# Loading each 4 MB tile of the K and V caches as two transfers of 64 partitions in a one-core attention decode step

## The chip, the core and the metric

The kernel runs on one core of a Trainium2 chip. The metric is the device time of one execution in microseconds; before the change it is 378.08 us, the median of 3 runs (378.05 to 378.56). The profile is one further execution of the same program, with its own span.

## The reference

One decode step for four sequences: layer norm, attention of 32 query heads over 16 cached key/value heads in a window of the last 4096 positions, a residual, a second layer norm and a gated feed-forward layer. What matters here is the size of the caches' window: 4 sequences x 16 heads x 4096 positions x 128 values of two bytes are 67 MB of K and as much of V. Both are read once.

```python
def _A_ref(x, k_cache, v_cache, wq, wo):
    W = min(4096, max(256, Sk // 4))          # 4096 of Sk = 16384
    rep = Hq // Hkv                           # 32 // 16
    q = (x @ wq).reshape(B, Sq, Hq, Dh).transpose(0, 2, 1, 3)
    k = jnp.repeat(k_cache[:, :, Sk - W:, :], rep, axis=1)
    v = jnp.repeat(v_cache[:, :, Sk - W:, :], rep, axis=1)
    scores = jnp.einsum("bhqd,bhkd->bhqk", q, k) * (Dh ** -0.5)
    p = _softmax(scores, axis=-1)
    o = jnp.einsum("bhqk,bhkd->bhqd", p, v)
    return o.transpose(0, 2, 1, 3).reshape(B, Sq, Hq * Dh) @ wo

h = x + _A_ref(_layernorm(x), A_k_cache, A_v_cache, A_wq, A_wo)
h2 = h + _B_ref(_layernorm(h), B_W_gate, B_W_up, B_W_down)   # (relu(h W_gate) * (h W_up)) W_down
```

## The kernel before

The caches are worked on in 16 tiles of K and 16 tiles of V (`NTILE`). Tile g holds four heads of one sequence (g // 4 is the sequence). It is 128 partitions x 16384 values of two bytes, 4 MB, and comes by a single transfer (lines 235 to 242). Partition 4p + a holds positions 128p to 128p + 127 of the window of head a of the four, so one partition's row is one unbroken run of 32 KB in the cache.

A tile lives in one of four slots (`NSLOT`) of a big buffer, `arena`, in a ring (`ring_slot`, line 229). The order of the loads is wq, K tiles 0 to 3, then K tile g and V tile g - 4 in turn, and V tiles 12 to 15 (lines 251 to 264). Then the weights of the output projection and of the feed-forward layer follow, in the same buffer (lines 265 to 284). All of these are issued by SP on one queue, in this order. `place` (line 216) records which 64-value blocks of the arena a load overwrites, and makes the load wait for the last instruction that reads them: the scores of the earlier K tile, `("QK", g)`, or the weighted sum of the earlier V tile, `("PV", g)`.

The order on each engine is that of the program text. `Prog.emit` (line 71) gives every instruction that somebody waits for a semaphore value. For a transfer the value of its semaphore grows by 16 (line 92), one for each of the 16 DMA engines; each slot has one semaphore (`slot0` to `slot3`). A wait that an engine has already made is not made again (line 108).

On the computing side a K tile is first rearranged in place by VectorE (`turn_k`, line 418; the transpose is line 422), and then TensorE makes the scores (`pe_qk`, lines 425 to 448, and the helper at line 34). A V tile goes straight to TensorE (`pe_pv`, line 492, whose matmuls are line 507 and line 34). Between them lie the softmax (lines 450 to 489) and the selection of the valid part of the product (`select_o`, lines 512 to 525). The weights need TensorE alone and a few small operations on VectorE and ScalarE (lines 606 to 702).

The small input x comes by a transfer of its own, 4 partitions of 1152 bytes, issued by ScalarE (line 335).

Of the kernel before, what the change touches and what calls it, by code (L numbers as in the profile page):

```python
# [16 lines left out]
SK = 16384  # L17
WIN = 4096
# [7 lines left out]
TILE = 16384  # L26
# [94 lines left out]
def bass_sequential_preLN__sliding_block_cached__glu_gated_reglu__decode_kernel(  # L121
# [12 lines left out]
    with ExitStack() as es:  # L134
        cnt = [0]

        def sb(name, shape, dt):
            return es.enter_context(nc.sbuf_tensor("sb_" + name, shape, dt))

        P = Prog()  # L140
# [8 lines left out]
        arena = sb("arena", [128, AW], BF16)  # L149
# [66 lines left out]
        def place(name, off, size, reader, make, key=None):  # L216
            deps = []
            for blk in range(off // 64, (off + size) // 64):
                r = owner.get(blk)
                if r is not None and r not in deps:  # L220
                    deps.append(r)
                owner[blk] = reader
            semk = key or "d_" + "_".join(str(v) for v in name)
            P.dma("sync", ("L",) + name, make, semk, deps)
            land[name] = off

        ring = [(-1 - 2 * NTILE) % NSLOT]
# [1 line left out]
        def ring_slot():  # L229
            s = ring[0] % NSLOT  # L230
            ring[0] += 1
            return s


        def add_kv(kind, g):
            b, qd = divmod(g, 4)
            s = ring_slot()
            off = slot0 + s * TILE
            cache = A_k_cache if kind == "K" else A_v_cache
            src = cache[b, 4 * qd:4 * qd + 4, SK - WIN:SK, :].rearrange("a (p t) d -> p a (t d)", p=32)  # L240
            place((kind, g), off, TILE, ("QK", g) if kind == "K" else ("PV", g),
                  lambda e: e.dma_start(out=arena[:, off:off + TILE], in_=src), key=f"slot{s}")  # L242


        def main_rows(W):
            return W[0:512, :].rearrange("(p r) n -> p (r n)", r=4)

        def last_rows(W):
# [3 lines left out]
        s = ring_slot()  # L252
        wq_off = slot0 + s * TILE
        place(("wq", 0), wq_off, TILE, "QMM",
              lambda e: e.dma_start(out=arena[:, wq_off:wq_off + TILE], in_=main_rows(A_wq)), key=f"slot{s}")  # L255
        for g in range(NTILE):
            add_kv("K", g)
            if g >= 4:
                add_kv("V", g - 4)
# [3 lines left out]
        for g in range(NTILE - 4, NTILE):  # L263
            add_kv("V", g)
        place(("wo",), WO_OFF, H * D, "WO",
              lambda e: e.dma_start(out=arena[:, WO_OFF:WO_OFF + H * D], in_=A_wo.rearrange("(p r) n -> p (r n)", p=128)))
        gu_off = {}
        off = WO_OFF + H * D
        for g, W in ((0, B_W_gate), (1, B_W_up)):
            for m, n, src in ((4, F // 2, last_rows(W)), (0, 3 * F, main_rows(W)[:, 0:3 * F]), (3, F, main_rows(W)[:, 3 * F:4 * F])):  # L270
                if g == 0 and m == 0:
                    n, src = 4 * F, main_rows(W)
# [7 lines left out]
        for r0, r1 in zip(WD_ROWS, WD_ROWS[1:]):  # L280
            place(("wd", r0), wd_off + r0 * D, (r1 - r0) * D, ("DOWN", 1),
                  lambda e, r0=r0, r1=r1: e.dma_start(  # L282
                      out=arena[:, wd_off + r0 * D:wd_off + r1 * D],
                      in_=B_W_down.rearrange("(p r) n -> p (r n)", p=128)[:, r0 * D:r1 * D]))
# [18 lines left out]
                                                in_=c_qm[:, :, :].rearrange("p q (h j) -> p q h j", j=4),  # L303
# [4 lines left out]
                                                in_=to_v[:, :, :].rearrange("p n (k a) -> p n k a", a=4),  # L308
# [14 lines left out]
        for sg in range(2):  # L323
            pool(f"c_toq{sg + 1}", lambda e, sg=sg: e.affine_select(
                out=toq[:, :, :, :], in_=toq[:, :, :, :],
# [213 lines left out]
        def finish_o():  # L539
            for q in range(4):  # L540
                for qd in range(4):
# [17 lines left out]
                                              in_=bass.AP(tensor=e8, offset=0, ap=[[8, 128], [0, 4], [1, 8]])), ["c_e8", "c_selc0"])  # L559
# [47 lines left out]
        for a in range(8):  # L607
            for n in range(2):
                for j in range(4):
# [4 lines left out]
                    else:  # L614
# [6 lines left out]
                                             in_=bass.AP(tensor=psb, offset=512 + 224, ap=[[4096, 128], [1, 64], [0, 2]])), ["part1"])  # L621
# [27 lines left out]
        for g in range(2):  # L649
            for c in (4, 0, 1, 2, 3):  # L650
                part_ = c if c == 4 or (c == 3 and g) else 0
                for m in range(3):
                    for j in range(4):
                        first = m == 0 and j == 0 and (c in (0, 4) or part_ == 3)
                        deps = [("L", "gu", g, part_)] if first else []
# [20 lines left out]
        for i in range(2):  # L676
            dve(("HHT", i), lambda e, i=i: e.transpose(
                out=hhT[:, 576 * i:576 * i + 576].rearrange("p (r q) -> p r q", q=32),
                in_=bass.AP(tensor=pp, offset=3712 + 18 * i, ap=[[PPW, 128], [1, 18], [36, 32]])), [("HH", m) for m in range(3)])
# [12 lines left out]
        for r in range(36):  # L692
            for n in range(2):
                deps = []
# [9 lines left out]
        for n in range(2):  # L704
            lo, hi = ncol[n]
            P.dma(("sync", "scalar")[n], ("O", n), lambda e, n=n, lo=lo, hi=hi: e.dma_start(
                out=orow[:, lo:hi], in_=out_sb[32 * n:32 * n + 4, 0:hi - lo]),
# [31 lines left out]
```

## Time and profile before

| What | Value |
|---|---|
| median of 3 runs | 378.08 us |
| span of the profiled execution | 376.5 us |
| mean TensorE clock granted | 0.79 |
| read from HBM in the span | 159.58 MB, 424 GB/s |
| of these, K and V | 32 transfers of 4096 KB |
| VectorE waiting for K tiles (line 422) | 66.5 us in 16 waits |
| SP waiting for TensorE before loads of line 242 | 237.4 us in 24 waits, the longest 17.4 us |

The profile's page gives busy times and shares by engine, the span in 40 slices, the DMA queues, and the chain of work that ended last. A line such as "L422 DVE" is an instruction of VectorE from line 422 of the program; PE is TensorE, SPq the issuing of transfers by SP. "A <-B" behind an idle time says that the engine was waiting for B. The trace has further records behind the page: for every DMA packet its start, length, size and queue, and for every transfer the sixteen moments at which its semaphore was raised, one by each DMA engine, here called its landings. Times are from the start of the span.

### The profile page before, as it was taken

How to read it: one execution, taken by the hardware profiler on the slowest of the kernel's cores; microseconds unless marked ns; L12 is line 12 of the kernel's file. 1: busy time of each engine (PE TensorE's matmuls, PEld its weight loads, DVE VectorE, ACT ScalarE, POOL GpSimd, SP SyncE). 2: the span in 40 equal slices, each digit the busy share in tenths (PEclk: the TensorE clock that was granted, in tenths of full speed). 3: DMA queues.
4: the chain of work that ended last, by engine and by line, in shares of the span. 5: the costliest groups of instructions: out<-in, count | busy, mean ns of one | idle time of the engine just before them, and what ended most of it. 6: DMA issues, size and time to landing. Idle time of an engine off the chain costs nothing.

```text
span 376.5 us, 2541 instructions
## 1 busy us (share of the span) xinstructions
PE 209.2 (56%) x1447; PEld 39.2 (10%) x694; DVE 227.6 (60%) x164; ACT 53.8 (14%) x84; POOL 10.7 (3%) x29
## 2 busy tenths in 40 slices
PE   0404443249919091749282844664555687776748
PEld 0000000001101010101010100110000101003305
DVE  3088878779292959584847778665659423342140
ACT  3093000211000114010101140101010401121010
POOL 8300000000000000000000000000000000000000
PEclk9975666659979687788778885968596989996688
DMA  8999999999999999999999999999999999999996
GB/s 335 446 435 432 413 446 446 425 411 446 444 421 414 443 444 421 414 446 446 421 413 446 446 418 421 438 446 418 425 439 446 413 432 435 430 423 426 437 414 263
DMA packets 6514, 159.74 MB, mean 424 GB/s; under 512 B 736, under 2 KB 872, under 8 KB 1512
## 3 DMA queue, kind: packets, MB, share of 16 engines
q1 hardware_dynamic: 6488, 159.58, 98.8%
q8 instruction: 8, 0.13, 0.1%
q10 hardware_dynamic: 16, 0.01, 0.0%
q14 instruction: 2, 0.02, 0.0%
HBM read 159.58 MB, written 0.00 MB: 424 GB/s over the span
## 4 chain that ended last, share of the span: by engine, by line
DMA 62%; DVE 18%; PE 18%; SPq 1%; issue 1%; ACT 0%
DMA sb_arena<-in_A_k_cache_dram 53%; DVE sb_arena L422 16%; PE psb L34 11%; DMA sb_arena<-in_B_W_down_dram 9%; PE psb L446 4%; PE psb L507 2%; DVE sb_o_tmp L520 1%; DVE sb_pp L485 1%; PE psb L685 0%; SPq L242 0%; PE psb L473 0%; SPq L282 0%; ACT sb_out_sb L702 0%; SPq L255 0%; SPq L251 0%
## 5 line engine op out<-in xcount | busy, mean ns | idle before, releaser
L422 DVE STREAM_TRANSPOSE sb_arena<-sb_arena 128x8192 f32<-128x8192 f32 (+1 forms) x19 | 139.9, 7365 | 66.5 <-DMA sb_arena<-in_A_k_cache_dram 66.5
L446 PE MATMUL psb<-sb_arena 128*32 128x512 bf16 x256 | 42.5, 629 | 119.1 <-DVE sb_arena L422 119.0
L34 PE MATMUL psb<-sb_arena,sb_pp 128*128 128x512 bf16 x382 | 105.2, 383 | 2.7 <-issue 2.6
L507 PE MATMUL psb<-sb_arena,sb_pp 128*128 128x512 bf16 x115 | 44.1, 383 | 8.9 <-DVE sb_o_tmp L520 8.9
L34 PE MATMUL psb<-sb_arena 128*32 128x512 bf16 x256 | 44.2, 649 | 0.0
L517 ACT COPY sb_o_tmp<-psb 32x512 f32<-32x512 f32 x32 | 18.5, 577 | 179.3 <-PE psb L34 179.1
L520 DVE TENSOR_TENSOR sb_o_tmp<-psb,sb_fm 32x512 f32<-32x512 f32 x32 | 21.7, 678 | 16.9 <-PE psb L34 16.4
L446 PEld LDWEIGHTS psb<-sb_arena 128*32 128x32 bf16 x256 | 9.6, 119 | 161.4 <-DVE sb_arena L422 132.2
L507 PEld LDWEIGHTS psb<-sb_arena,sb_pp 128*128 128x128 bf16 x128 | 12.6, 99 | 113.4 <-issue 113.4
L524 DVE TENSOR_REDUCE sb_o_sel<-sb_o_tmp 128x128 f32<-128x512 f32 x16 | 17.7, 1106 | 0.5
L465 ACT ACTIVATE sb_pp<-psb,sb_hx 128x1024 bf16<-128x1024 f32 x4 | 4.5, 1113 | 78.4 <-DVE sb_hx L462 78.4
L485 DVE TENSOR_TENSOR sb_pp<-psb,sb_m 128x1024 bf16<-128x1024 f32 x8 | 9.4, 1209 | 4.5 <-PE psb L473 4.5
L480 ACT ACTIVATE sb_pp<-psb,sb_m 128x512 bf16<-128x512 f32 x16 | 9.7, 692 | 14.8 <-PE psb L473 14.8
L523 DVE TENSOR_TENSOR sb_o_tmp<-sb_o_tmp,sb_fm 64x512 f32<-64x512 f32 x16 | 11.0, 690 | 0.5
L413 ACT COPY sb_arena<-sb_q_keep 32x256 bf16<-32x256 bf16 x8 | 9.7, 1452 | 0.1
L685 PE MATMUL psb<-sb_arena,sb_pp 128*32 128x352 bf16 (+1 forms) x72 | 7.6, 349 | 3.7 <-DMA sb_arena<-in_B_W_down_dram 3.6
L399 DVE CAST sb_pp<-psb 128x512 bf16<-128x512 f32 x1 | 2.4, 2426 | 11.3 <-PE psb L379 11.3
L468 DVE STREAM_TRANSPOSE sb_pp<-sb_pp 128x1024 bf16<-128x1024 bf16 x4 | 5.0, 1246 | 5.1 <-ACT sb_pp L465 5.1
L473 PE MATMUL psb<-sb_pp,sb_to_v 128*32 128x256 bf16 x64 | 4.3, 401 | 6.2 <-DVE sb_pp L468 6.2
L673 DVE TENSOR_TENSOR sb_pp<-psb,sb_pp 128x384 bf16<-128x384 f32 x3 | 1.5, 551 | 9.0 <-PE psb L664 9.0
L379 PE MATMUL psb<-sb_arena,sb_xnT 128*32 128x512 bf16 x16 | 2.6, 628 | 7.2 <-DMA sb_arena<-in_A_wq_dram 7.2
L664 PE MATMUL psb<-sb_arena,sb_hnT 128*32 128x384 bf16 x40 | 4.2, 405 | 3.9 <-DVE sb_hnT L645 2.0
(119 smaller groups left out, 88.1 us busy)
## 6 DMA issues: line engine op xcount, KB each, us to landing
sb_arena<-in_A_k_cache_dram SPq DMA_DIRECT2D x16, 4096.0 KB, 26.2
sb_arena<-in_A_v_cache_dram SPq DMA_DIRECT2D x16, 4096.0 KB, 28.5
sb_arena<-in_A_wo_dram SPq DMA_DIRECT2D x1, 4608.0 KB, 26.2
sb_arena<-in_B_W_gate_dram SPq DMA_DIRECT2D x1, 4608.0 KB, 29.3
sb_arena<-in_A_wq_dram SPq DMA_DIRECT2D x1, 4096.0 KB, 12.9
sb_arena<-in_B_W_up_dram SPq DMA_DIRECT2D x1, 3456.0 KB, 30.3
sb_arena<-in_B_W_down_dram SPq DMA_DIRECT2D x1, 2160.0 KB, 29.6
sb_arena<-in_B_W_down_dram SPq DMA_DIRECT2D x1, 1440.0 KB, 32.6
```

The costliest lines, as they stand in the source:

```text
L34: return e.add_instruction(mybir.InstMatmult(name=e.bass.get_next_instruction_name(), engine=mybir.EngineType.PE, ins=[e.lower_ap(rhs), e. ...
L413: act("QW", lambda e, i=i, q=q: e.copy(out=bass.AP(tensor=arena, offset=32 * i * AW + 2 * i + q, ap=[[AW, 32], [512, 16], [136, 4], [32, 4]]),
L422: dve(("TRA", g), lambda e: e.transpose(out=dst, in_=src), [("L", "K", g)] if lo == 0 else [])
L446: fn = lambda e, out_=out_, lhsT=lhsT, rhs=rhs, start=start, stop=stop: e.matmul(out_, lhsT=lhsT, rhs=rhs, start=start, stop=stop, skip_gr ...
L480: act(("EV", b, 0), lambda e, a=a: e.activation(out=bass.AP(tensor=pp, offset=2 * a, ap=[[PPW, 128], [8, 2], [32, 128], [1, 2]]), in_=bank ...
L485: dve(("EV", b, 1), lambda e, n=n: e.tensor_tensor(out=bass.AP(tensor=pp, offset=16 + 8 * n, ap=[[PPW, 128], [32, 128], [2, 4], [1, 2]]), ...
L507: fn = lambda e, lhsT=lhsT, rhs=rhs, k=k, j=j: e.matmul(bank[2 + j], lhsT=lhsT, rhs=rhs, start=(k == 0), stop=(k == 7), skip_group_check=True)
L517: act(("OSC", g), lambda e, j=j: e.copy(out=o_tmp[32 * j:32 * j + 32, 0:512], in_=bank[2 + j][32 * j:32 * j + 32, :]), [("PV", g), ("OSEL" ...
L520: dve(("OSD", g), lambda e, j=j: e.tensor_tensor(out=ot(32 * j, 32), in0=bank[2 + j][32 * j:32 * j + 32, :].rearrange("p (t d) -> p t d", ...
L523: dve(("OS", g), lambda e: e.tensor_tensor(out=ot(64, 64), in0=ot(64, 64), in1=fmb(64, 64), op=ALU.mult), [("OSC", g)])
L524: dve(("OSEL", g), lambda e: e.tensor_reduce(out=o_sel[:, qd, b, :], in_=o_tmp[:, 0:512].rearrange("p (t d) -> p d t", d=DH), axis=AX.X, o ...
L685: return lambda e: e.matmul(bank[n][32 * n:32 * n + 32, 0:hi - lo], lhsT=lhsT, rhs=w[:, lo:hi], start=start, stop=stop, skip_group_check=True)
```

## The change

`add_kv` makes two transfers of each tile: partitions 0 to 63 and then partitions 64 to 127, each 2 MB. The rearrangement of the source is split into h (which half), p (16 in place of 32) and t, so each partition gets the same row of the cache as before. `place` takes a list of transfers as well as a single one; the transfers of a list are put on SP's queue one after the other with the same dependencies and the same semaphore. The name of the load stands for the second of them, whose semaphore value counts both (32 for a tile). The loads of the weights and of x are as they were.

```diff
@@ def place(name, off, size, reader, make, key=None):
             semk = key or "d_" + "_".join(str(v) for v in name)
-            P.dma("sync", ("L",) + name, make, semk, deps)
+            for one in make if isinstance(make, list) else [make]:
+                P.dma("sync", ("L",) + name, one, semk, deps)
             land[name] = off
@@ def add_kv(kind, g):
-            src = cache[b, 4 * qd:4 * qd + 4, SK - WIN:SK, :].rearrange("a (p t) d -> p a (t d)", p=32)
+            src = cache[b, 4 * qd:4 * qd + 4, SK - WIN:SK, :].rearrange("a (h p t) d -> h p a (t d)", h=2, p=16)
             place((kind, g), off, TILE, ("QK", g) if kind == "K" else ("PV", g),
-                  lambda e: e.dma_start(out=arena[:, off:off + TILE], in_=src), key=f"slot{s}")
+                  [lambda e, h=h: e.dma_start(out=arena[64 * h:64 * h + 64, off:off + TILE], in_=src[h])
+                   for h in range(2)], key=f"slot{s}")
```

## The prediction

> **What bounds the kernel now.** I read the busy slices and the DMA queues first, then the chain of waits, then single lines. The page:
>
> ```profile
> span 376.5 us, 2541 instructions
> PE 209.2 (56%) x1447; PEld 39.2 (10%) x694; DVE 227.6 (60%) x164; ACT 53.8 (14%) x84; POOL 10.7 (3%) x29
> DMA  8999999999999999999999999999999999999996
> ...
> q1 hardware_dynamic: 6488, 159.58, 98.8%
> ...
> DMA 62%; DVE 18%; PE 18%; SPq 1%; issue 1%; ACT 0%
> ```
>
> No compute engine is busy for more than 60% of the span. The queue that carries every load has its sixteen DMA engines in work for 98.8% of it. So the kernel lasts as long as its bytes take; the DVE and PE pieces of the chain are the path by which a buffer comes free for the next load, not work that delays the bytes. Busy times by stretch, with the granted clock, the DMA share and the rate as the last three columns, agree:
>
> ```profile
> core 0: us, PE busy (x) PEld busy (x) DVE busy (x) ACT busy (x) POOL busy (x), PEclk, DMA share, GB/s
> ...
> 64.00:160.00 96.00, 54.99 (x357) 8.08 (x159) 67.63 (x41) 12.36 (x22) 0.00 (x0) 0.77 1.00 431
> 160.00:326.00 166.00, 101.42 (x580) 14.04 (x231) 104.68 (x70) 19.40 (x34) 0.00 (x0) 0.81 1.01 433
> ```
>
> The rate is the same whatever the clock and the other engines do. The pace of one tile shows in VectorE's first transposes, each of which starts when its K tile has landed:
>
> ```profile
> 23.91 8.71 DVE L422 STREAM_TRANSPOSE sb_arena<-sb_arena 128x8192 f32<-128x8192 f32 x1 [1.03 <-DMA sb_arena<-in_A_k_cache_dram]
> 33.61 8.71 DVE L422 STREAM_TRANSPOSE sb_arena<-sb_arena 128x8192 f32<-128x8192 f32 x1 [0.99 <-DMA sb_arena<-in_A_k_cache_dram]
> 43.33 8.71 DVE L422 STREAM_TRANSPOSE sb_arena<-sb_arena 128x8192 f32<-128x8192 f32 x1 [1.00 <-DMA sb_arena<-in_A_k_cache_dram]
> ```
>
> 9.7 us apart. The landing records give it for all 32 K and V tiles: the first engine is done with wq at 13.62 us and with the last V tile at 324.44 us, 310.82 / 32 = 9.713 us a tile. The packet records say why: one row of a tile is one packet of 32768 bytes, its median time is 1.216 us and its shortest 1.213; 128 rows over 16 engines are 8 packets an engine, 8 x 1.216 = 9.73 us. Packets stand end to end. From the last V tile (all engines at 326.19 us) to the end, the weights queued behind it take 48 us and the close about 2 us.
>
> How deep the queue is decides what SP's issues cost:
>
> ```profile
> L242 SPq DMA_DIRECT2D sb_arena<-in_A_k_cache_dram x16: 534/535/692, 1.7 to 251.4; - x16
> L242 SPq DMA_DIRECT2D sb_arena<-in_A_v_cache_dram x16: 534/535/536, 46.3 to 297.4; - x16
> ...
> DMA to landing us min/median/max: 17.9/26.5/40.2
> ```
>
> An issue takes 0.535 us, and its tile lands 17.9 us later at the least. Of these the tile's own transfer is 9.7, so at least 8.2 us of earlier packets lie ahead of any issue.
>
> **The change, part by part.** Removed: 32 transfers of 128 rows. Added: 64 transfers of 64 rows, with the same bytes, the same rows of the cache to the same partitions, and the same 32 KB packets. Nothing moves on TensorE, VectorE, ScalarE or GpSimd.
>
> SP: 32 more issues of 0.535 us and the step of 0.04 us between issues in the chain, 18.4 us of SP's time. Cover: SP waits 237.4 us for PE at line 242 alone, and the second half needs no wait of its own, since both halves have the same dependencies. A second half goes out 0.58 us late against at least 8.2 us of queued packets, so 0. Behind it on SP stand only later loads. Without that cover it would be the whole 18.4 us.
>
> Semaphores: each transfer ends on each engine with a 4-byte packet of 9 ns. 32 more of them are 0.3 us on every engine. The consumers wait for the sum of both halves (32 a tile), so no transpose or matmul starts sooner than now.
>
> The packets: this is the term that decides, and no K or V row of the trace shows it. A transfer of 64 rows, if it is spread over 16 engines as the transfer of 128 is, has 4 rows an engine, and all sixteen engines write into one half of the partitions at once. The lower end: the limit of 1.216 us sits in the engine that sends. Then a half tile takes 4.86 us and the tile 9.73 as before, cost 0. The instruction fetches of 8192 bytes ahead of the kernel, which don't go to the arena, took 307 ns, 26.7 GB/s, nearly the 26.9 GB/s of 32768 / 1.216. That fits a sender's limit. The upper end: the limit sits where the rows are received, and belongs to a group of partitions. 16 x 26.9 = 431 GB/s into 128 partitions are 3.4 GB/s a partition; 64 partitions take 216 GB/s, a packet 2.43 us, a tile 19.4 us. The nearest row with few partitions is x, 4 rows of 1152 bytes: its four packets took 146, 255, 102 and 48 ns on four engines, all between 2.85 and 3.16 us, so 4608 bytes in 0.305 us, 15.1 GB/s for four engines, 3.8 GB/s a partition. Packets of the same size in the last W_down load, into 128 partitions, took 51 ns. x comes at the start, where other packets are slow too (4096 bytes in 159 to 656 ns), so it is a hint, no measurement. But its rate lies beside the upper end's and a quarter of what four senders alone would give, and I take the upper end.
>
> The upper end has a discount. Two engines that share a receiver lose nothing while one of them is already in the other half. If one leads its partner by w us of work, a half tile costs 2 x 4.86 - w. The sixteen engines finish the first K tile within 0.54 us of each other, two engines taken at random 0.2 us apart; at the last V tile it is 1.75 and 0.82 us, since each of eight 16 KB instruction fetches (about 1.07 us) held up one engine more. A tile is ready when its slowest pair is, so I take the small lead: 64 x 0.2 = 13 us. With 0.82 it would be 52, with 1.75 it would be 112.
>
> [...]
>
> Where the stall goes: into VectorE's wait for K. The first K tile would land near 33 instead of 23.9 us, and the computation of a tile (8.7 us of transpose, 4 us of scores) hides under a load of 19 us, so the next buffer is always free in time and the queue stays full: three tiles lie ahead of each issue. After the last V tile the same weights follow at the same rate, full transfers of 128 rows, 48 us. PE is then ahead of its work of now, not behind.
>
> Sum, against the profiled span: 376.5 + 310.8 (every tile twice as long) - 13 + 0.3 = 674.6. The median lies 378.08 - 376.5 = 1.6 us above the span, so 676 us.
>
> **The rivals.** (B) The receiver is shared, but the engines fall out of step by several us, because one of a pair is favoured or is held up by fetches, and half tiles overlap in part. For it: the spread of landings grows from 0.54 to 1.75 us through the run, and the queue is deep enough that a leader isn't stopped. Against: engines differ only by whole fetch stalls, packets otherwise agree within 1%, and a leader that runs out of issued tiles waits for its partner, which sets them level again. With a lead of half a half tile, 2.43 us, the cost is 310.8 - 64 x 2.43 = 155, time 533 us; the case reaches from 379 to 577.
>
> (C) The packet's limit is the sender's. For it: the 26.7 GB/s of the instruction fetch, and 1.213 us as a hard floor in 4224 packets. Against: x. The time is 378.08 + 0.3 = 378.4 us, not slower by what can be measured. It decides wherever the first half tile lands within 5 us of the transfer ahead of it. That the change doesn't do what it says, since the queue joins both halves, has the same time.
>
> (D) Shorter bursts keep the packets at their floor: 32 tiles x 8 x (1.216 - 1.213) = 0.8 us, time 377.3, faster. Nothing speaks for it but that the floor exists.
>
> **How the numbers follow.** Doubling (577 to 698): 0.62. B: 0.20. C: 0.14. D: 0.04. The forecast is 676 us. Its own range ends above at the full doubling, 376.5 + 310.8 + 0.3 + 1.6 = 689.2, and with each of eight fetches holding up the slowest pair (8 x 1.07 = 8.6) at 698; below at the discount for 1.75 us, 577. To hold 8 in 10, I go down through B to 400, which leaves out C, D and about a tenth of B: 0.62 + 0.18 = 0.80. A measurement of this kernel can tell 0.2%, 0.76 us, from no change. Faster by that: 0.04; within: 0.14; slower: 0.82.
>
> **What would show it.** If right: 32768-byte packets near 2.4 us, the rate near 220 GB/s from the first K tile to the last V tile and 430 after it, the DMA share still at 1.00, transposes of the first K tiles some 19 us apart, K landing some 60 us after issue, and VectorE's wait for K well above its 66.5 us in sum. If packets stay at 1.216 us, the receiver isn't the limit and I am wrong altogether. If packets are bimodal, 1.2 and 2.4, the engines fall out of step and B holds. If the DMA share falls, SP's issues have come onto the path, which I have costed at nothing.

## The result, and the profile after

The changed kernel takes 699.62 us, the median of 4 runs (690.62 to 703.73), against 378.08 (378.05 to 378.56). The comparison, from which disturbed runs are left out, gives a ratio of 1.8333 (95% interval 1.8284 to 1.8382). The profiled execution has a span of 695.2 us, 318.7 us more than before.

The page of the changed kernel: the span, the busy times, the busy share of the DMA engines and the rate in 40 slices, and the queue of the loads.

```profile
span 695.2 us, 2588 instructions
PE 240.0 (35%) x1462; PEld 41.5 (6%) x694; DVE 228.5 (33%) x164; ACT 53.6 (8%) x84; POOL 10.5 (2%) x29
DMA  9999999999999999999999999999999999999997
GB/s 332 213 211 222 216 217 211 215 213 210 211 211 211 212 213 214 211 219 219 211 217 212 213 211 211 217 214 217 211 217 215 213 210 211 215 213 214 420 416 332
...
q1 hardware_dynamic: 7000, 159.59, 99.5%
```

No compute engine has become the limit: VectorE has 228.5 us of work in place of 227.6, and TensorE's 240.0 us in place of 209.2, at a lower granted clock (0.69 in place of 0.79), are 35% of the span. The DMA engines are as full as they were, and move half as much in a microsecond. The low rate begins after the first slice (wq is a whole transfer) and ends in the 38th, where the weights, again whole transfers, come at 420 GB/s. The busy share alone would not have shown anything; it has to be read beside the rate.

The transposes of the first K tiles, from the timeline of VectorE in the changed kernel (start, duration, and in brackets the idle time before and who ended it), and below it VectorE's wait for K in sum, times and longest, and the issues of line 243 (242 before):

```profile
33.80 8.71 DVE L424 STREAM_TRANSPOSE sb_arena<-sb_arena 128x8192 f32<-128x8192 f32 x1 [11.40 <-DMA sb_arena<-in_A_k_cache_dram]
53.52 8.71 DVE L424 STREAM_TRANSPOSE sb_arena<-sb_arena 128x8192 f32<-128x8192 f32 x1 [11.01 <-DMA sb_arena<-in_A_k_cache_dram]
```

```profile
DVE sb_arena L424 <- DMA sb_arena<-in_A_k_cache_dram: 335.4, 16, 27.3
```

```profile
L243 SPq DMA_DIRECT2D sb_arena<-in_A_k_cache_dram x32: 536/594/662, 1.7 to 480.8; - x32
...
DMA to landing us min/median/max: 22.2/60.1/75.6
```

The tiles are 19.7 us apart, where they were 9.7. A half tile lands 60.1 us after its issue in the median, and 22.2 us at the least, and the DMA share is 1.00 from 64 to 640 us, so the queue never runs dry and the doubled number of issues stays hidden.

The packet records hold the whole difference. Each engine carries 256 packets of 32768 bytes for K and V. Their mean was 1.2174 us and is now 2.4603 us: 256 x 1.2429 = 318.2 us, and the span has grown by 318.7.

### The profile page after: what moved, and what is told of

Read it like the earlier page. It is cut to its first block, busy times and chain, and to the rows that moved or that the text cites. A ratio compares the mean times of both kernels' runs of the same rounds, so it can differ in the third digit from the quotient of the medians.

```text
span 695.2 us, 2588 instructions
## 1 busy us (share of the span) xinstructions
PE 240.0 (35%) x1462; PEld 41.5 (6%) x694; DVE 228.5 (33%) x164; ACT 53.6 (8%) x84; POOL 10.5 (2%) x29
## 4 chain that ended last, share of the span: by engine, by line
another core or an unknown queue 52%; DVE 25%; DMA 12%; PE 10%; ACT 1%; SPq 0%; issue 0%
DVE sb_arena L424 19%; DMA sb_arena<-in_A_k_cache_dram 7%; PE psb L34 6%; DMA sb_arena<-in_B_W_down_dram 5%; PE psb L509 2%; DVE sb_o_tmp L522 2%; DVE sb_o_sel L526 1%; PE psb L687 1%; DVE sb_pp L487 1%; PE psb L448 1%; DVE sb_o_tmp L525 1%; DVE sb_pp L470 1%; DVE sb_hx L453 1%; ACT sb_pp L467 1%
## 5 line engine op out<-in xcount | busy, mean ns | idle before, releaser
L448 PE MATMUL psb<-sb_arena 128*32 128x512 bf16 x256 | 44.0, 636 | 293.0 <-DVE sb_arena L424 293.0
L34 PE MATMUL psb<-sb_arena,sb_pp 128*128 128x512 bf16 x384 | 127.3, 449 | 0.0
L509 PE MATMUL psb<-sb_arena,sb_pp 128*128 128x512 bf16 x128 | 58.3, 455 | 113.2 <-DMA sb_arena<-in_A_v_cache_dram 113.2
L34 PE MATMUL psb<-sb_arena 128*32 128x512 bf16 x256 | 45.0, 644 | 0.0
L509 PEld LDWEIGHTS psb<-sb_arena,sb_pp 128*128 128x128 bf16 x128 | 14.5, 113 | 244.4 <-DMA sb_arena<-in_A_v_cache_dram 132.2
L526 DVE TENSOR_REDUCE sb_o_sel<-sb_o_tmp 128x128 f32<-128x512 f32 x16 | 17.6, 1102 | 0.5
L487 DVE TENSOR_TENSOR sb_pp<-psb,sb_m 128x1024 bf16<-128x1024 f32 x8 | 9.3, 1207 | 14.1 <-PE psb L475 14.1
L666 PE MATMUL psb<-sb_arena,sb_hnT 128*32 128x384 bf16 x40 | 4.2, 405 | 6.4 <-DMA sb_arena<-in_B_W_up_dram 4.4
L34 PE MATMUL psb<-sb_arena,sb_hnT 128*32 128x384 bf16 x80 | 6.1, 389 | 0.0
L453 DVE TENSOR_REDUCE sb_hx<-psb 128x1 f32<-128x1024 f32 x4 | 4.9, 1224 | 2.0 <-PE psb L34 2.0
```

The costliest lines, as they stand in the source:

```text
L34: return e.add_instruction(mybir.InstMatmult(name=e.bass.get_next_instruction_name(), engine=mybir.EngineType.PE, ins=[e.lower_ap(rhs), e. ...
L448: fn = lambda e, out_=out_, lhsT=lhsT, rhs=rhs, start=start, stop=stop: e.matmul(out_, lhsT=lhsT, rhs=rhs, start=start, stop=stop, skip_gr ...
L453: dve(("MAX", b), lambda e: e.tensor_reduce(out=hx[:, 0:1], in_=psb[:, 0:2, :].rearrange("p a b -> p (a b)"), axis=AX.X, op=ALU.max, negat ...
L487: dve(("EV", b, 1), lambda e, n=n: e.tensor_tensor(out=bass.AP(tensor=pp, offset=16 + 8 * n, ap=[[PPW, 128], [32, 128], [2, 4], [1, 2]]), ...
L509: fn = lambda e, lhsT=lhsT, rhs=rhs, k=k, j=j: e.matmul(bank[2 + j], lhsT=lhsT, rhs=rhs, start=(k == 0), stop=(k == 7), skip_group_check=True)
L526: dve(("OSEL", g), lambda e: e.tensor_reduce(out=o_sel[:, qd, b, :], in_=o_tmp[:, 0:512].rearrange("p (t d) -> p d t", d=DH), axis=AX.X, o ...
```

## The experiments

The theory, which no trace shows by itself: a packet is slow because two DMA engines write at once to the same receiving part of the buffer. Two, because the packets took twice as long (2.4603 us in the mean, before 1.2174); sixteen engines that all write into partitions 0 to 63 would then share eight such entrances, and sixteen that write into partitions 64 to 127 eight others. Three things are assumed for the sums below: that the two are engines e and e + 8, that 32 neighbouring partitions reach all eight entrances of their half, and that in a transfer of 64 rows engine e carries rows 4e to 4e + 3. The records don't number the engines, and "engines 0 to 7" stands here for the eight that a transfer on eight engines uses. The rivals: the number or the size of the transfers costs the time; any transfer of 64 rows is slow; the limit belongs to each partition; the order in which rows are read from HBM has changed; VectorE's wait for K is at fault.

**Two transfers of all partitions.** The tile is split by columns.

```diff
-src = cache[...].rearrange("a (h p t) d -> h p a (t d)", h=2, p=16)
+src = cache[...].rearrange("a (p t) d -> p a (t d)", p=32)
+[... out=arena[:, off + h * QWW:off + h * QWW + QWW], in_=src[:, :, h * QWW:h * QWW + QWW] ... for h in range(2)]
```

> Each K or V tile by two transfers of all 128 partitions and half the columns (16 KB rows). Receiver theory (two engines share an entrance to the partitions): packets of 16384 bytes at about 0.61 us, tile 9.73 us, time 378 to 380 us, since the count of transfers costs only 9 ns a transfer and engine. Rival, the number of transfers or their 2 MB size costs: about 690 us as with the halves by partition.

Measured 380.18 us, ratio 1.0059 (1.0042 to 1.0075). As many transfers of the same 2 MB as in the change cost 2 us. Packets of 16384 bytes take 0.615 us in the mean, two of them 1.2299 against 1.2174 for one of 32768: 256 x 0.0125 = 3.2 us of engine time is more than the loss, so the shorter packets are enough to explain it. Number and size of the transfers are out.

**Other ranges of partitions.** In the first kernel a tile comes as partitions 32 to 95, 0 to 31, 96 to 127; in the second as four transfers of 32.

```diff
+[... out=arena[lo:lo + n, off:off + TILE], in_=src[lo // 4:(lo + n) // 4] ... for lo, n in ((32, 64), (0, 32), (96, 32))]
```

> Each tile by three transfers: partitions 32 to 95 (64 rows), then 0 to 31, then 96 to 127. Receiver theory with two halves of eight entrances, where 32 neighbouring partitions reach all eight of a half: partitions 32 to 95 reach sixteen, so 4 packets of 1.216 us (4.86 us), and each 32 rows are 2 packets of 2.515 us (5.03 us); tile 14.9 us in place of 9.71, 376.5 + 32 x 5.21 + 1.6 = 545 us. Rival, any transfer of 64 rows or fewer halves the rate: about 695 us. Rival, the limit belongs to each partition: 32 rows at a quarter of the rate, 4.86 x 2 + 2 x 9.7 = 29 us a tile, about 1000 us.

> Each tile by four transfers of 32 neighbouring partitions. Receiver theory with eight entrances in 32 neighbouring partitions: 8 packets of 2.515 us an engine as with halves, tile 20.1 us, about 700 us. Rival, the limit belongs to each partition (3.4 GB/s): packets near 4.9 us, tile 39 us, about 1310 us.

Measured 609.87 us (608.59 to 611.15) and 714.17 us (713.81 to 714.53). The second time looks like a hit and is none. Busy share and rate of the kernel with quarters, from its page, and the stretch from 64 to 500 us with the same two as its last columns:

```profile
DMA  7545544554455455445545544554554459889773
GB/s 324 221 206 221 221 215 211 221 221 212 215 221 219 208 220 221 213 213 219 221 208 219 221 215 212 218 217 211 219 221 215 210 235 206 257 246 220 289 315 166
```

```profile
core 0: us, PE busy (x) PEld busy (x) DVE busy (x) ACT busy (x) POOL busy (x), PEclk, DMA share, GB/s
64.00:500.00 436.00, 139.39 (x764) 19.17 (x330) 150.83 (x81) 23.19 (x41) 0.00 (x0) 0.66 0.50 216
```

Half the engines are idle, and the packets are fast: 1.213 us in the median, not 2.515. A transfer of 32 rows ran on eight engines: its 128 transfers of K and V left no more of the 4-byte semaphore packets than the change's 64 did, 8 each in place of 16. The first dimension of its source pattern, p, is 8; for the halves of the change, which ran on sixteen, it is 16.

This miss is of use. Eight engines working alone bring 216 GB/s into 32 partitions, 6.8 GB/s a partition, twice the 3.4 GB/s that my upper end had taken as a partition's limit. And it is the rate that sixteen engines reach in the change with a share of 1.00. So the limit belongs neither to a partition nor to the number of rows. That eight engines don't slow each other there fits what was assumed of 32 neighbouring partitions. The first kernel is muddied by the same fact: its 32-row pieces, counted in the same way, put 12 packets of a tile on engines 0 to 7 and 4 on the others. 12 x 1.216 would be 14.6 us a tile; with a mean packet of 1.464 us it is 17.6, which gives 376.5 + 32 x 7.9 = 629; 610 was measured, so this is a rough account. 72% of its packets are under 1.3 us.

**One trace with both.** All tiles come whole but two.

```diff
+cuts = {("K", 0): ((0, 64), (64, 64)), ("K", 2): ((32, 64), (0, 32), (96, 32))}.get((kind, g), ((0, 128),))
```

> All tiles by one transfer but two: K tile 0 by partitions 0 to 63 and 64 to 127, K tile 2 by partitions 32 to 95, then 0 to 31, then 96 to 127 (these two go over eight engines). Receiver theory: the 64-row transfers of tile 0 have packets near 2.5 us, the 64-row transfer of tile 2, on the same sixteen engines, has packets of 1.216 us, since its engines e and e + 8 write into different halves. Rival, a transfer of 64 rows is slow wherever it goes: 2.5 us in both. Time about 378 + 10 + 5 = 393 us.

Measured 398.57 us, one run. That is 5.6 us above the expected time; the four packets of tile 2 that turned out to be shared, 4 x 1.21 us, were not in that sum. Its stretches, chosen by the packet records (DMA share and rate are last):

```profile
core 0: us, PE busy (x) PEld busy (x) DVE busy (x) ACT busy (x) POOL busy (x), PEclk, DMA share, GB/s
14.00:33.00 19.00, 5.04 (x48) 1.30 (x32) 3.78 (x8) 12.52 (x11) 0.00 (x0) 1.00 0.98 207
35.50:43.00 7.50, 0.00 (x0) 0.00 (x0) 7.50 (x1) 0.00 (x0) 0.00 (x0) 1.00 0.97 419
43.50:48.00 4.50, 3.79 (x32) 0.56 (x16) 3.70 (x1) 0.00 (x0) 0.00 (x0) 1.00 0.95 408
48.50:52.50 4.00, 0.00 (x0) 0.00 (x0) 4.00 (x1) 0.00 (x0) 0.00 (x0) 0.84 1.01 434
54.00:61.50 7.50, 2.93 (x28) 0.32 (x8) 0.00 (x0) 0.00 (x0) 0.00 (x0) 0.73 0.96 208
```

The first line is tile 0 by halves: packets of 2.54 us in the median. The second is tile 1, whole: 1.218. The third is the 64-row transfer to partitions 32 to 95: 1.216 us. Same number of rows, same sixteen engines (DMA share 0.98 and 0.95), same packet size, and twice the speed, only because the rows lie across the middle. That a transfer of 64 rows is slow as such is out.

The last two lines hold a second such pair. Engines 0 to 7 load partitions 0 to 31 and then 96 to 127, while engines 8 to 15 have gone on to the next whole tile. First nothing is slow (1.218 us), then every packet takes 2.425 us: by the theory the partner writes the other half in the one stretch and the same half in the other. Which engines load what here, and that engines 8 to 15 take partitions 64 to 127 of a whole tile, isn't in the trace; it is inferred.

**Putting the engines out of step.** If two engines of a pair collide because they are in the same half at the same time, a pair of which one lags by half a tile's share (four packets) never collides, with every transfer of 64 rows left as in the change. Only K tile 0 is cut in another way, so that engines 0 to 7 get more of its rows than engines 8 to 15. A first attempt cut it with a 32-row transfer:

```diff
+if kind == "K" and g == 0:
+    parts = [... out=arena[96:128], in_=src[24:32] ...]
+    parts += [... out=arena[a:32:4], in_=src[0:8, a] ... for a in range(4)]
+    parts += [... out=arena[32 + a:96:4], in_=src[8:24, a] ... for a in range(4)]
```

> Halves of 64 partitions as in the change, but K tile 0 is cut so that engines 0 to 7 get 10 of its rows and engines 8 to 15 get 6: the first eight stand four packets (half a tile's share) behind from then on. Receiver theory, the two engines of an entrance being e and e + 8: while one writes the lower half the other writes the upper, nothing is shared, packets 1.216 us, tile 9.73 us; 378 + 2.4 for the uneven first tile + 2.4 for its shared part + 0.3 = 383 us. Receiver theory with other pairs (neighbours): about 695 us. Rival, transfers of 64 rows, their count, or the order in which rows are read from HBM cost the time: about 695 us, since all of these are as in the change.

Measured 698.12 us, ratio 1.8464 (1.8429 to 1.8499). The expectation rested on a wrong count. The 32-row transfer, too, ran on engines 0 to 7 alone, so they got 12 packets and the others 4: a lag of eight, a whole tile, at which both engines are by the theory again in the same half. The landings bear this out: of the second tile in one slot eight engines' landings begin at 108.11 us and the other eight's at 127.77, a tile's 19.7 us later. The next three kernels keep to transfers of 8, 16 and 64 rows; m of the four groups of 16 rows in partitions 0 to 63 go as two transfers of 8 rows, taken to run on engines 0 to 7 as in the first attempt.

```diff
+if kind == "K" and g == 0:
+    cuts = [(u, 8, a) for a in range(m) for u in (0, 8)] + [None] + [(0, 16, a) for a in range(m, 4)]
+    parts = [parts[1] if c is None else ... out=arena[4 * u + a:4 * u + 4 * n:4], in_=src[u:u + n, a] ... for c in cuts]
```

> Control: halves as in the change, but K tile 0 comes as partitions 64 to 127 and then four transfers of 16 rows (every fourth partition of 0 to 63), one row an engine; all engines get 8 rows, no lag. Receiver theory and rivals alike: packets 2.515 us, about 697 us, within the scatter of the changed kernel (690 to 704).

> As the control, but 16 rows of K tile 0 go by two transfers of 8 rows, which only engines 0 to 7 carry: 9 rows for them, 7 for engines 8 to 15, a lag of two packets. Receiver theory with pairs e and e + 8: of a half tile's four packets two are shared (2.515 us) and two alone (1.216 us), 7.46 us, tile 14.9 us, 376.5 + 32 x 5.2 + about 3 = 546 us. Rival (count, size or HBM order of the transfers): about 697 us. Rival, the engines fall back into step: between 546 and 697 us, with landings closing up through the run.

> As the control, but 32 rows of K tile 0 go by four transfers of 8 rows: 10 rows for engines 0 to 7, 6 for engines 8 to 15, a lag of four packets, half a tile's share; this is what e4_lag4 was meant to be. Receiver theory: one of a pair writes the lower half while the other writes the upper, nothing is shared, packets 1.216 us, 378 + 2.4 for the uneven split + 2.6 for two shared packets = about 383 us. Rivals (count, size or HBM order of the transfers): about 697 us.

| lag at the start | expected | measured |
|---|---|---|
| 0 packets (m = 0) | 697 us | 699.55 and 700.00 us |
| 2 packets (m = 1) | 546 us | 568.60 and 578.93 us |
| 4 packets (m = 2) | 383 us | 438.39, 447.94, 469.40 and 570.92 us |
| 8 packets (the first attempt) | 383 us, taken for 4 | 698.12 us |

Going from no lag to four takes off 130 to 260 us and eight gives it all back, though each of these kernels has the same 64-row transfers of tiles 1 to 15 of K and all of V, in the same order and from the same addresses. That the order of reading HBM is slow in itself is out, and two engines that slow each other stand one in each group of eight. The lag was made for the pairs e and e + 8; other pairs across the two groups would give the same times.

One rival of that kind is left. In every run a row's partition and its address go together (the 32 KB at 32 KB x p of a head's window go to partition 4p + a), so reads that collide in HBM at particular addresses would give the same pairs as writes that collide in the buffer, and a lag would keep both apart. Against it: in the probe the two engines of a pair read as far apart in the fast transfer (partitions 32 to 95) as in the slow ones, 8 x 32 KB = 256 KB. And wq, whose 128 rows also lie 32 KB apart, must have engines 256 KB apart too, if its rows are dealt as those of a whole tile are thought to be; its packets took 1.22 us. No run sent the same rows to other partitions, so that the collision is at the receiving end is well supported, and not shown by itself.

But the times with a lag are above the expectation and scatter. The stretches of the kernel with a lag of four (469.40 us), cut at its 16 KB instruction fetches (at 52.4, 110.4, 160.3, 229.3 and 285.5 us):

```profile
core 0: us, PE busy (x) PEld busy (x) DVE busy (x) ACT busy (x) POOL busy (x), PEclk, DMA share, GB/s
30.00:52.00 22.00, 7.89 (x64) 1.58 (x32) 19.31 (x3) 1.46 (x2) 0.00 (x0) 0.58 0.98 407
56.00:110.00 54.00, 25.55 (x186) 4.33 (x93) 37.30 (x19) 4.96 (x9) 0.00 (x0) 0.69 1.01 398
113.00:160.00 47.00, 23.45 (x135) 2.97 (x49) 27.07 (x16) 3.51 (x6) 0.00 (x0) 0.75 1.00 363
163.00:229.00 66.00, 27.63 (x169) 4.12 (x68) 38.29 (x20) 5.06 (x10) 0.00 (x0) 0.69 1.00 341
232.00:285.00 53.00, 24.05 (x148) 3.09 (x64) 29.27 (x19) 6.23 (x11) 0.00 (x0) 0.71 1.01 348
```

Up to the first fetch the theory holds nearly in full: 407 GB/s with halves that run at 213 in step. Of a half's four packets three take 1.218 us and one 1.39. The first fetch takes 1.06 us, and 1.1 us after its start come the first packets of 2.46 and 1.96 us. They are two of sixteen that start between 53.4 and 53.9 us; the other fourteen take 1.47 to 1.49. So one pair alone has fallen back, and what is limited belongs to a pair of engines and not to a whole half. After most later fetches the rate is lower again. So the lag isn't kept. That a fetch throws one pair out of its lag fits the first one, in time and in number of packets; for the later ones, and for the scatter between runs, it is argued and not shown.

**Half of the change.**

```diff
+cuts = ((0, 64), (64, 64)) if kind == "K" else ((0, 128),)
```

> The change undone for V: K tiles by halves, V tiles by one transfer. Receiver theory: each halved tile costs (695.2 - 376.5) / 32 = 9.96 us, wherever it stands in the queue, so 378.1 + 16 x 9.96 = 537.4 us. If the cost came through the wait of VectorE for K, all of the 318.7 us would stay, about 697 us.

> The change undone for K: V tiles by halves, K tiles by one transfer. Receiver theory: 537.4 us again. If the cost came through the wait of VectorE for K, about 378 us.

Measured 544.19 and 566.81 us with only K halved, 565.51 and 592.72 with only V. Both are above the half, 537, the more so with V, and neither is near 378 or 697. The wait of VectorE for K isn't the cause: without a single K tile in halves the loss is at least as large. The two runs of each kernel lie 23 and 27 us apart, so the 20 us between the two kernels are not clear of the scatter; nothing further was tried on them.

No version beats the kernel before. If engines 8 to 15 take partitions 64 to 127 of a whole tile, as inferred above, whole transfers, whose packets took 1.216 us, already give each engine an entrance of its own in the sense of the theory.

## Why the prediction came out as it did

The direction and the range held, and the runs support the mechanism; the size was 676 us, and 699.62 came, and 674.6 for the span, where 695.2 came. By its own steps:

- What bounds the kernel: right. The span grew by 318.7 us, the packets of each engine by 318.2.
- SP's 32 issues at no cost: right. The DMA share stayed at about 1.00 for as long as K and V came.
- 9 ns for each semaphore packet: too low. The mean was 9.0 ns before, and 17.5 in the changed kernel for as long as K and V came: 64 x 17.5 - 32 x 9.0 = 832 ns, 0.8 us on every engine in place of 0.3. The kernel with as many whole transfers lost 2 us in all, which would cover either.
- The packets, from two ends: I took the upper, and that was right, but the reason that led to it was wrong in part. I had put it in the receiver, for a group of partitions that two engines can share, which the runs bear out, but worked out its size as a rate for each partition and leaned on the x transfer's 3.8 GB/s. That reading of x was weak: its 15.1 GB/s are about a seventh of four senders at 26.9 GB/s, not a quarter as I wrote, so x fits neither end well. The kernel with quarters has 6.8 GB/s a partition. The runs fit a limit in an entrance that two engines share (2.515 us for a packet with sixteen engines on 64 partitions, 1.213 with eight on 32); with sixteen engines on 64 partitions both readings give the same rate.
- The size: "16 x 26.9 = 431 GB/s into 128 partitions are 3.4 GB/s a partition; 64 partitions take 216 GB/s, a packet 2.43 us". This is the term that was mis-sized. The trace has 214 GB/s from 64 to 640 us, and a packet that is taken for fully shared took 2.515 us (the median), 0.083 more than twice 1.216: 256 x 0.083 = 21.2 us, nearly all of the gap of 20.6 between the forecast span and the measured one. Why sharing cost 3.4% beyond the doubling stays open; in the probe a shared packet took 2.54 us in one stretch and 2.425 in another.
- The discount for engines out of step: 13 us forecast. That two engines share a receiver was assumed there; no row of the trace before shows it. The mean packet lies 0.055 us under the median, which is taken for the fully shared one, 256 x 0.055 = 14.1 us. It also held through the whole run, although landings in one tile spread by up to 2.1 us; that the slowest pair sets the pace fits, and was not tested by itself.
- The tail after the last V tile: 48 us of weights and the close; from its last landing at 644.4 us to the end it is 50.8 us, before 50.3.

Of the rivals, the sender's limit is refuted by the 2.5 us packets, and the faster one with it. Out of step, rival B, is a real effect, but the changed kernel starts in step, and single stalls (its eight 16 KB instruction fetches took 1.07 to 1.38 us) didn't build up a lag of four packets in it. In the kernels that were given a lag, times came between 438 and 579 us, about the region that B was priced for (379 to 577).

## What to carry to other kernels

When a load is bound by its DMA engines, look at the time of one packet and at the rate beside the busy share: here the share was 1.00 at 214 GB/s with packets of 2.515 us, as it was at 431 GB/s with packets of 1.216. The load in pieces kept its rate when each piece spanned all 128 partitions (by columns: 0.6% lost), and lost half of it (214 GB/s in place of 431) when the pieces were partitions 0 to 63 and 64 to 127. Before cutting a load by rows, find out on how many engines each piece will run: pieces of 32 rows ran on eight here (DMA share 0.50).

## What the runs showed of the hardware beyond that

- A transfer of 32 rows whose source pattern begins with a dimension of 8 ran on eight engines: DMA share 0.50 at 216 GB/s.
- Partitions 32 to 95 took a transfer of 64 rows at full rate (408 GB/s, packets of 1.216 us), partitions 0 to 63 at half (207 GB/s, 2.54 us).
- A lag between DMA engines, set once at the start, sped up the stream of transfers behind it: 407 GB/s up to the first instruction fetch, against 213 without a lag. It is no tool: the rate fell within the run (398, 363, 341 and 348 GB/s in the next stretches), and the four times of one kernel went from 438 to 571 us.
